# First-layer layer norm of chunks 1 and 2 issued ahead of the K and Q evictions, its rstd on ScalarE, w1/w2 loaded early, one DMA transpose per chunk

## The chip, the cores and the metric

The kernel runs on one core of a Trainium2 chip. The metric is the device time of one execution in microseconds (us); less is better. Line numbers such as L523 are lines of the kernel before.

## The reference

The input `x` has 2048 rows of 512 bf16 values. Four layers are applied to it in turn, each as x = x + f(layernorm(x)): attention, feed-forward, attention, feed-forward, with the same weights in both pairs.

```python
x = x + _A_ref(_layernorm(x), A_wqkv, A_wo)   # linear attention, 32 heads of 16
x = x + _B_ref(_layernorm(x), B_w1, B_w2)     # relu(h @ w1) @ w2, 512 -> 1376 -> 512
# ... and both once more
# in _A_ref: phi(t) = where(t > 0, t + 1, exp(t)) + 1e-6, on q and k
#   kv = sum_s phi(k) v;  z = sum_s phi(k);  out = (phi(q) kv) / (phi(q) z + 1e-6) @ wo
```

## The kernel before

The 2048 rows are 16 tiles of 128 rows, in four chunks of four tiles. Everything stays in SBUF; only the inputs and the result move to and from HBM. An attention layer has two stages.

**First stage.** For each tile: layer norm to `xn`, its transpose to `Tb`, the K projection (`a_k`: four 512-column matmuls into one PSUM bank); for each chunk: four Q projections (`a_q`, one bank each). Each K or Q bank is evicted by `phi_evac` in four instructions: on ScalarE (ACT) an identity with bias into `big` (L506) and an exp into `escr` (L508); on VectorE (DVE) a min into `emscr` (L510, "em") and a max in `big` (L516, "phi"). `escr` and `emscr` have 6 slots each (`NSCR`). From phi(K) come z (`a_z`, one-column matmuls) and G (`a_g`, 256-column matmuls of `xn` with phi(K); 128 matmuls in all).

**Second stage ("bar").** z becomes `Zc` (L557); `a_den` makes the denominators, whose reciprocals (L616, L618) are spread over partitions by 12 DMAs (`a_spread`, L628) and multiplied into phi(Q) (`a_pqs`, L637, "pqs"). G becomes KV (L590, two halves) and with `wo` becomes `Mf` (`a_m`, L597/L598; two pairs of matmuls called M pairs here). Then `a_fin_mm` computes the output ("fin"), L534 adds the residual, and `ln_next` makes the layer norm and the transposes of the next layer. The feed-forward layers (`b_h`, `b_out`) follow chunk by chunk.

**The first layer's norm.** Chunk 0 goes tile by tile (`ln_own`). For chunks 1 to 3, `ln_first` issues four `bn_stats` (L427, "bst"), four `bn_aggr` (L428), one `veps` (L435), then rstd as a power on GpSimd (POOL, L448), an `nbias` on DVE (L451) and four norms (L463, on ACT or DVE as the scheduler picks). Chunks 0 and 1 are transposed on TensorE (PE) through `transpose_pe` (L494, four matmuls a tile, "trp") and copied out of PSUM by ACT or DVE (L498/L499, "trev"); chunks 2 and 3 by a DMA transpose each (L479). In later layers all chunks go by DMA transpose; chunk 0 of the layer after an attention goes as two halves.

**What sets the order.** The code only lists operations with what they read and write, and a guessed cost. `_list_schedule` (L123) then simulates the engines and fixes one order per engine; each engine runs its list strictly in that order and waits on semaphores. A look-ahead of `WINDOW` operations in listing order, the guessed costs and the eight PSUM banks decide who goes first, so moving a call such as `ln_first` in the listing, or changing a guessed cost, re-orders all engines. `p1(t)` lists `ln_first(t + 1)` ahead of the K projections of chunk t. All DMAs, loads and transposes alike, are issued by SyncE (SP) on one queue. `ld_ff` (L382) holds the loads of `w1` and `w2` back until the transposed chunks 2 and 3 have landed; the first DMA transpose waits for `wk`, `wq`, `wv` and `wo` (`ALL_LOADS`).

```python
def p1(t):                                  # L823
    if first_layer and t + 1 < NCH:
        ln_first(t + 1)
        if t + 2 == NCH:
            ld_ff()
    for i in range(4 * t, 4 * t + 4):
        a_k(i)
```

Of the kernel before, what the change touches and what calls it, by code (L numbers as in the profile page):

```python
# [22 lines left out]
C_ACT_EXP = 495.0  # L23
C_DVE_FLEX = 600.0
# [13 lines left out]
C_POOL_NORM = 900.0  # L38
# [211 lines left out]
def build_kernel(nc, A_x, A_wqkv, A_wo, B_w1, B_w2, out, n_layers_pairs=2, K_STT=0, Q_STT=0, A_PE_CHUNKS=0, windows=None,  # L250
# [20 lines left out]
    with es:  # L271
# [25 lines left out]
        NSCR = 6  # L297
        escr = sb("escr", [128, NSCR, 512], BF16)
        emscr = sb("emscr", [128, NSCR, 512], BF16)
# [68 lines left out]
        def ld_x(t, lo=0):  # L368
            dma(lambda e, t=t: e.dma_start(xin[:, 4 * t + lo:4 * t + 4, :], x_v[:, 4 * t + lo:4 * t + 4, :]),
                [], [("xin", i) for i in range(4 * t + lo, 4 * t + 4)], 1500.0, "ld_x%d" % t)  # L370
        dma(lambda e: e.dma_start(xin[:, 0, :], x_v[:, 0, :]), [], [("xin", 0)], 100.0, "ld_x0a")
        wq_v = A_wqkv.rearrange("(c p) n -> p c n", p=128)
        ld_x(0, 1)
# [8 lines left out]
        def ld_ff():  # L382
            after = [("T", i) for i in range(4 * FIRST_PE_CHUNKS, NT)]
            dma(lambda e: e.dma_start(w1[:], B_w1.rearrange("(c p) n -> p c n", p=128)), after, [("w1",)], 4000.0, "ld_w1")
            dma(lambda e: e.dma_start(w2[:, 0:nfull, :], B_w2[0:nfull * 128, :].rearrange("(c p) n -> p c n", p=128)),
                after, [("w2a",)], 3800.0, "ld_w2a")
            if FLAST < 128:
                dma(lambda e: e.dma_start(w2[0:FLAST, NFC - 1, :], B_w2[nfull * 128:DFF, :]), after, [("w2b",)], 600.0, "ld_w2b")
        W2KEYS = [("w2a",), ("w2b",)] if FLAST < 128 else [("w2a",)]
        ALL_LOADS = [("wk",), ("wv",), ("wq",), ("wo",)]  # L390
# [39 lines left out]
        def ln_chunk(t, first):  # L430
            sl = slice(4 * t, 4 * t + 4)
            tl = range(4 * t, 4 * t + 4)
            if first:
                mean_ap = mv[:, sl, 0]
                g.add(DVE, lambda e: e.tensor_scalar(veps[:, sl], mv[:, sl, 1], 0.0, EPS, ALU.max, ALU.add),  # L435
                      [("var", i) for i in tl], [("veps", t)], C_DVE_SMALL, name="veps%d" % t)
            else:
                g.add(POOL, lambda e: e.tensor_scalar(mean[:, sl], s1[:, sl], -INV_D, None, ALU.mult),  # L438
                      [("s1", i) for i in tl], [("mean", i) for i in tl], C_POOL_SMALL, name="nmean%d" % t)
                g.add(POOL, lambda e: e.tensor_tensor(nm2[:, sl], s1[:, sl], mean[:, sl], ALU.mult),  # L440
                      [("s1", i) for i in tl] + [("mean", i) for i in tl], [("nm2", t)], C_POOL_SMALL, name="msq%d" % t)
                g.add(POOL, lambda e: e.tensor_scalar(nm2[:, sl], nm2[:, sl], D * EPS, None, ALU.add),
                      [("nm2", t)], [("nm2", t)], C_POOL_SMALL, name="msqe%d" % t)
                g.add(POOL, lambda e: e.tensor_tensor(var[:, sl], s2[:, sl], nm2[:, sl], ALU.add),
                      [("s2", i) for i in tl] + [("nm2", t)], [("var", i) for i in tl], C_POOL_SMALL, name="var%d" % t)
                g.add(POOL, lambda e: e.tensor_scalar(veps[:, sl], var[:, sl], INV_D, EPS, ALU.mult, ALU.max),
                      [("var", i) for i in tl], [("veps", t)], C_POOL_SMALL, name="veps%d" % t)
            g.add(POOL, lambda e: e.tensor_tensor(rstd[:, sl], veps[:, sl], nhalf[:, 0:4], ALU.pow),  # L448
                  [("veps", t), ("nhalf",)], [("rstd", t)], C_POOL_POW, name="rstd%d" % t)
            if first:  # L450
                g.add(DVE, lambda e: e.scalar_tensor_tensor(nbias[:, sl], mean_ap, -1.0, rstd[:, sl], ALU.mult, ALU.mult),  # L451
                      [("mean", i) for i in tl] + [("rstd", t)], [("nbias", t)], C_DVE_SMALL, name="nbias%d" % t)
            else:
                g.add(POOL, lambda e: e.tensor_tensor(nbias[:, sl], mean[:, sl], rstd[:, sl], ALU.mult),
                      [("mean", i) for i in tl] + [("rstd", t)], [("nbias", t)], C_POOL_SMALL, name="nbias%d" % t)

        def ln_norm(i, first):
            t = i // 4
            if first:
                src, rd = xin[:, i, :], [("xin", i), ("rstd", t), ("nbias", t)]  # L460
                alts = [(ACT, lambda e: e.activation(xn[:, i, :], src, ACTF.Identity, scale=rstd[:, i:i + 1], bias=nbias[:, i:i + 1]),
                         C_ACT_SB_AP),
                        (DVE, lambda e: e.tensor_scalar(xn[:, i, :], src, rstd[:, i:i + 1], nbias[:, i:i + 1], ALU.mult, ALU.add),  # L463
                         C_DVE_NORM_BF)]
                g.add_flex(alts, rd, [("xn", i)], name="norm%d" % i)
                return
            src = xres[:, i, :]
            if i % 4 == 2:
                g.add(ACT, lambda e: e.activation(xn[:, i, :], src, ACTF.Identity, scale=rstd[:, i:i + 1], bias=nbias[:, i:i + 1]),
                      [("xres", i), ("rstd", t), ("nbias", t)], [("xn", i)], C_ACT_SB_AP, name="norm%d" % i)  # L470
                return
            eng, cost = (POOL, C_POOL_NORM) if i % 4 == 3 else (DVE, 500.0)
            g.add(eng, lambda e: e.tensor_scalar(xn[:, i, :], src, mean[:, i:i + 1], rstd[:, i:i + 1], ALU.add, ALU.mult),  # L473
                  [("xres", i), ("rstd", t), ("mean", i)], [("xn", i)], cost, name="norm%d" % i)

        def transpose_chunk(t, extra_reads=(), parts=1):
            n = 4 // parts
            for i0 in range(4 * t, 4 * t + 4, n):
                dma(lambda e, i0=i0: e.dma_start_transpose(Tb[:, i0:i0 + n, :, :].rearrange("p i c t -> p (i c) t"),  # L479
                                                           xn[:, i0:i0 + n, :].rearrange("p i d -> p (i d)")),  # L480
                    [("xn", i) for i in range(i0, i0 + n)] + list(extra_reads),
                    [("T", i) for i in range(i0, i0 + n)], 2300.0 if parts == 1 else 1050.0, "tr%d_%d" % (t, i0 % 4),
                    issue=1200.0)

        def transpose_pe(i):
# [5 lines left out]
            def _emit(e, i=i):  # L491
                last = None
                for c in range(4):
# [5 lines left out]
                        (DVE, lambda e: e.tensor_copy(dst, psb()[:, :]), C_DVE_FLEX)],  # L499
                       [("ps", b)], [("T", i)], name="trev%d" % i)  # L500

        def phi_evac(b, dst_ap, dst_key, name, stt):
            s = scr_state["e"]
            scr_state["e"] = (s + 1) % NSCR
            if not stt:
# [4 lines left out]
            g.add(DVE, lambda e: e.tensor_scalar(emscr[:, s, :], escr[:, s, :], 1.0, 1e-6, ALU.min, ALU.add),  # L510
                  [("escr", s)], [("emscr", s)], C_DVE_BF4X, name=name + "_em")
            if stt:
                g.add(DVE, lambda e: e.scalar_tensor_tensor(dst_ap, psv[:, b, :], 1.0 + 1e-6, emscr[:, s, :], ALU.add, ALU.max),
                      [("ps", b), ("emscr", s)], [dst_key], C_DVE_PSUM, name=name + "_phi")
            else:
                g.add(DVE, lambda e: e.tensor_tensor(dst_ap, dst_ap, emscr[:, s, :], ALU.max),  # L516
# [283 lines left out]
        def ln_next(t, on_pe=False, parts=1):  # L800
# [5 lines left out]
            if not on_pe:  # L806
                tr_dma(t, parts)
# [217 lines left out]
```

## Time and profile before

| what | value |
|---|---|
| median of 3 runs | 291.74 us (291.61 to 292.29) |
| the profiled execution | 291.64 us, of which the span is 289.9 us |
| matmuls | 1696, PE busy 280.1 us (97% of the span) |
| ACT, DVE, POOL busy | 170.3, 139.6, 53.2 us |
| granted TensorE clock | 1.0 |
| DMA | 21.98 MB, of which 7.01 MB read from HBM |

PE's busy time hardly tells how much of the span is useful: matmuls are pipelined, and a row that stays open counts as busy. The spacing of the starts tells more: in a full stretch a 512-column matmul starts every 0.216 us (40 of them from 75.78 to 84.42 us) and a 256-column one about every 0.108 us. Where the starts lie further apart, PE waited. The views used below are the timeline of each engine (start, duration, line and count), the waits, and the time from issue to landing of each DMA.

### The profile page before, as it was taken

What the parts mean: (1) busy time and instruction counts of PE and PEld (TensorE: products, weight loads), DVE (VectorE), ACT (ScalarE), POOL (GpSimd) and SP (SyncE); (2) the same over time, 40 slices, a digit from 0 to 9 for tenths busy, and PEclk for the clock granted to TensorE, in tenths of its full rate; (3) what the DMA queues carried; (4) which work ended last, traced back from release to release, by engine and by line L of the source; (5) the groups of instructions that cost most, each with busy time, mean ns of one, the idle gap of its engine ahead of it and who ended that gap; (6) DMA issues with size and microseconds to landing.
All of it is one profiled execution on the core that took longest, in us unless ns stands there. A gap on an engine that the chain in (4) does not pass through costs nothing.

```text
span 289.9 us, 4431 instructions
## 1 busy us (share of the span) xinstructions
PE 280.1 (97%) x1696; PEld 143.4 (49%) x1696; DVE 139.6 (48%) x379; ACT 170.3 (59%) x352; POOL 53.2 (18%) x119
## 2 busy tenths in 40 slices
PE   7989899999899999999999999999999999999996
PEld 2456455644454454454455456674445445444444
DVE  4888856589800252260545387487971020020132
ACT  4888488738666285397554599843987605316000
POOL 5223100007800053040040320000880000000000
DMA  6900389661940007021003060281282005102012
GB/s 196 379 7 8 65 116 347 121 171 35 110 93 18 2 19 145 3 55 36 0 2 72 0 75 0 44 212 39 46 156 54 0 0 132 34 25 67 0 72 72
DMA packets 42790, 21.98 MB, mean 76 GB/s; under 512 B 34225, under 2 KB 40209, under 8 KB 42769
## 3 DMA queue, kind: packets, MB, share of 16 engines
q1 hardware_dynamic: 42768, 21.70, 32.6%
q8 instruction: 13, 0.21, 0.3%
q14 instruction: 9, 0.07, 0.1%
HBM read 7.01 MB, written 2.10 MB: 31 GB/s over the span
## 4 chain that ended last, share of the span: by engine, by line
PE 71%; DVE 11%; DMA 8%; ACT 4%; POOL 2%; SPq 1%; issue 1%; POOLq 0%
PE ps L523 71%; DMA Tb<-xn 4%; DVE xres L534 3%; DMA big<-rdc 3%; DVE bst L427 2%; POOL rstd L448 2%; ACT big L506 2%; DMA xin<-in_A_x_dram 1%; SPq L628 1%; ACT escr L508 1%; DVE big L637 1%; DVE xn L463 1%; ACT lnd L616 1%; DVE xn L473 1%; DVE big L516 1%
## 5 line engine op out<-in xcount | busy, mean ns | idle before, releaser
L523 PE MATMUL ps<-w,big 128*128 128x512 bf16 (+2 forms) x363 | 77.3, 372 | 0.0
L523 PE MATMUL ps<-Tb,w 128*128 128x512 bf16 x320 | 70.4, 379 | 0.0
L523 PEld LDWEIGHTS ps<-w,big 128*128 128x128 bf16 (+1 forms) x363 | 35.4, 98 | 40.7
L700 ACT ACTIVATE big<-ps 128x512 bf16<-128x512 f32 x74 | 44.1, 597 | 18.0 <-PE ps L523 17.9
L540 ACT ACTIVATE sqscr<-xres 128x512 bf16<-128x512 f32 x48 | 29.9, 624 | 33.6 <-DVE xres L534 33.4
L523 PEld LDWEIGHTS ps<-Tb,w 128*128 128x128 bf16 x320 | 30.8, 98 | 35.9
L506 ACT ACTIVATE big<-ps 128x512 bf16<-128x512 f32 x64 | 40.0, 626 | 9.6 <-PE ps L523 9.2
L534 DVE SCALAR_TENSOR_TENSOR xres<-ps,xres 128x512 f32<-128x512 f32 x32 | 21.1, 687 | 43.5 <-PE ps L523 43.5
L508 ACT ACTIVATE escr<-ps 128x512 bf16<-128x512 f32 x64 | 40.5, 633 | 0.0
L531 DVE TENSOR_TENSOR xin<-ps,xres 128x512 bf16<-128x512 f32 x15 | 10.4, 692 | 56.8 <-PE ps L523 56.8
L523 PE MATMUL ps<-big,xn 128*128 128x256 bf16 x256 | 31.8, 272 | 0.0
L523 PE MATMUL ps<-wqkv,Tb 128*128 128x512 bf16 x128 | 29.7, 379 | 1.0 <-DMA Tb<-xn 0.7
L510 DVE TENSOR_SCALAR emscr<-escr 128x512 bf16<-128x512 bf16 x64 | 18.5, 296 | 24.4 <-ACT escr L508 24.2
L523 PE MATMUL ps<-Tb,wqkv 128*128 128x512 bf16 x128 | 29.8, 379 | 0.1
L523 PE MATMUL ps<-Mf,big 128*128 128x512 bf16 x128 | 28.7, 379 | 0.0
L438 POOL TENSOR_SCALAR mean<-s 128x4 f32<-128x4 f32 x12 | 2.9, 239 | 136.8 <-DVE xres L534 136.8
L516 DVE TENSOR_TENSOR big<-big,emscr 128x512 bf16<-128x512 bf16 x64 | 26.9, 426 | 1.3
L523 PEld LDWEIGHTS ps<-big,xn 128*128 128x128 bf16 x256 | 23.8, 98 | 4.4 <-issue 0.9
L448 POOL TENSOR_TENSOR rstd<-veps,nhalf 128x4 f32<-128x4 f32 x15 | 17.7, 1177 | 20.6 <-DVE veps L435 19.6
L523 PEld LDWEIGHTS ps<-wqkv,Tb 128*128 128x128 bf16 x128 | 12.1, 98 | 15.2 <-ACT escr L508 1.2
L523 PEld LDWEIGHTS ps<-Mf,big 128*128 128x128 bf16 x128 | 12.2, 98 | 14.6 <-DVE Mf L598 0.8
L523 PEld LDWEIGHTS ps<-Tb,wqkv 128*128 128x128 bf16 x128 | 11.9, 98 | 13.5 <-ACT escr L508 0.4
(73 smaller groups left out, 198.8 us busy)
## 6 DMA issues: line engine op xcount, KB each, us to landing
big<-rdc SPq DMA_DIRECT2D x16, 128.0 KB, 2.7
big<-rdc SPq DMA_DIRECT2D x8, 256.0 KB, 4.7
wqkv<-in_A_wqkv_dram SPq DMA_DIRECT2D x3, 512.0 KB, 6.7
xin<-in_A_x_dram SPq DMA_DIRECT2D x3, 512.0 KB, 8.2
out_dram<-xin SPq DMA_DIRECT2D x3, 512.0 KB, 2.9
w<-in_B_w_dram SPq DMA_DIRECT2D x1, 1376.0 KB, 6.2
w<-in_B_w_dram SPq DMA_DIRECT2D x1, 1280.0 KB, 9.6
wo<-in_A_wo_dram SPq DMA_DIRECT2D x1, 512.0 KB, 10.2
```

Of the source, the lines that this page charges most:

```text
L427: g.add(DVE, lambda e: e.bn_stats(bst[:, i, :], xin[:, i, :]), [("xin", i)] + list(after), [("bst", i)], C_DVE_BNST, name="bnst%d" % i)
L438: g.add(POOL, lambda e: e.tensor_scalar(mean[:, sl], s1[:, sl], -INV_D, None, ALU.mult), [("s1", i) for i in tl], [("mean", i) for i in tl ...
L448: g.add(POOL, lambda e: e.tensor_tensor(rstd[:, sl], veps[:, sl], nhalf[:, 0:4], ALU.pow), [("veps", t), ("nhalf",)], [("rstd", t)], C_POO ...
L506: g.add(ACT, lambda e: e.activation(dst_ap, psv[:, b, :], ACTF.Identity, bias=1.0 + 1e-6, scale=1.0), [("ps", b)], [dst_key], C_ACT_PSUM, ...
L508: g.add(ACT, lambda e: e.activation(escr[:, s, :], psv[:, b, :], ACTF.Exp), [("ps", b)], [("escr", s)], C_ACT_EXP, name=name + "_exp")
L510: g.add(DVE, lambda e: e.tensor_scalar(emscr[:, s, :], escr[:, s, :], 1.0, 1e-6, ALU.min, ALU.add), [("escr", s)], [("emscr", s)], C_DVE_B ...
L516: g.add(DVE, lambda e: e.tensor_tensor(dst_ap, dst_ap, emscr[:, s, :], ALU.max), [dst_key, ("emscr", s)], [dst_key], 340.0, name=name + "_ ...
L523: last = e.matmul(o, l, r, start=st, stop=sp, skip_group_check=skip)
L531: g.add(DVE, lambda e: e.tensor_tensor(xin[:, i, :], psv[:, b, :], src, ALU.add), [("ps", b), skey], [("xin", i)], C_DVE_PSUM, name="resid ...
L534: g.add(DVE, lambda e: e.scalar_tensor_tensor(xres[:, i, :], psv[:, b, :], 0.0, src, ALU.add, ALU.add, accum_out=s1[:, i:i + 1]), [("ps", ...
L540: g.add(ACT, lambda e: e.activation(sqscr[:, q, :], xres[:, i, :], ACTF.Square, accum_out=s2[:, i:i + 1]), [("xres", i)], [("sqscr", q), ( ...
L700: g.add_flex([(ACT, lambda e, M=M, b=b, u=u: e.activation(unit_ap(u, M), psv[0:M, b, :], ACTF.Relu), C_ACT_PSUM), (DVE, lambda e, M=M, b=b ...
```

## The change

The layer norm of chunks 0, 1 and 2 is listed before the first K projection, that of chunk 3 after the K projections of chunk 0. In chunks 1 to 3 rstd is exp(-0.5 ln(var + eps)), two small activations on ACT in place of the power on POOL, and the norm is one DVE instruction (subtract mean, multiply by rstd) without `nbias`; chunk 1 goes in two halves of two tiles. `em` works in place in `escr`, which has 12 slots; `emscr` is gone. The loads of `w1` and `w2` are issued right after the other loads and wait for nothing. The first load brings two tiles of `x`, the second two. The DMA transpose of chunk 0 after an attention is one instruction, not two, and tile 3 of that chunk is normed on DVE, not on POOL. Some guessed costs differ.

```diff
-C_POOL_NORM = 900.0
+C_POOL_NORM = 1000.0
...
-        NSCR = 6
+        NSCR = 12
         escr = sb("escr", [128, NSCR, 512], BF16)
-        emscr = sb("emscr", [128, NSCR, 512], BF16)
...
-        dma(lambda e: e.dma_start(xin[:, 0, :], x_v[:, 0, :]), [], [("xin", 0)], 100.0, "ld_x0a")
+        dma(lambda e: e.dma_start(xin[:, 0:2, :], x_v[:, 0:2, :]), [], [("xin", 0), ("xin", 1)], 500.0, "ld_x0a")
...
-        def ld_ff():
-            after = [("T", i) for i in range(4 * FIRST_PE_CHUNKS, NT)]
-            dma(lambda e: e.dma_start(w1[:], B_w1.rearrange("(c p) n -> p c n", p=128)), after, [("w1",)], 4000.0, "ld_w1")
+        dma(lambda e: e.dma_start(w1[:], B_w1.rearrange("(c p) n -> p c n", p=128)), [], [("w1",)], 4000.0, "ld_w1")
...
-        ALL_LOADS = [("wk",), ("wv",), ("wq",), ("wo",)]
+        ALL_LOADS = [("wk",), ("wq",)]
...
+        def ln_part_first(lo, hi):
+            sl = slice(lo, hi)
+            tl = range(lo, hi)
+            g.add(DVE, lambda e: e.tensor_scalar(veps[:, sl], mv[:, sl, 1], 0.0, EPS, ALU.max, ALU.add),
+                  [("var", i) for i in tl], [("veps1", i) for i in tl], C_DVE_SMALL, name="veps%d" % lo)
+            g.add(ACT, lambda e: e.activation(var[:, sl], veps[:, sl], ACTF.Ln), [("veps1", i) for i in tl], [("lnv", lo)],
+                  C_ACT_TINY, name="lnv%d" % lo)
+            g.add(ACT, lambda e: e.activation(rstd[:, sl], var[:, sl], ACTF.Exp, scale=-0.5), [("lnv", lo)],
+                  [("rstd", i) for i in tl], C_ACT_TINY, name="rstd%d" % lo)
...
+        def ln_norm(i, first, urgent=False):
             if first:
+                g.add(DVE, lambda e: e.tensor_scalar(xn[:, i, :], xin[:, i, :], mv[:, i, 0:1], rstd[:, i:i + 1], ALU.subtract, ALU.mult),
+                      [("xin", i), ("mean", i), ("rstd", i)], [("xn", i)], C_DVE_NORM_BF, name="norm%d" % i)
                 return
...
-            eng, cost = (POOL, C_POOL_NORM) if i % 4 == 3 else (DVE, 500.0)
+            eng, cost = (POOL, C_POOL_NORM) if i % 4 == 3 and not urgent else (DVE, 460.0)
...
         def ln_first(t):
...
-            for i in range(4 * t, 4 * t + 4):
-                ln_stats_first(i)
-            ln_chunk(t, True)
+            step = 2 if t < FIRST_PE_CHUNKS else 4
+            for lo in range(4 * t, 4 * t + 4, step):
+                for i in range(lo, lo + step):
+                    ln_stats_first(i, [("veps1", lo - 1)])
+                ln_part_first(lo, lo + step)
...
-        ln_first(0)
+        for t in range(3):
+            ln_first(t)
...
                 def p1(t):
-                    if first_layer and t + 1 < NCH:
-                        ln_first(t + 1)
-                        if t + 2 == NCH:
-                            ld_ff()
                     for i in range(4 * t, 4 * t + 4):
                         a_k(i)
+                    if first_layer and t >= 0 and t + 3 < NCH:
+                        ln_first(t + 3)
...
-                    ln_next(t, t < A_PE_CHUNKS, 2 if t == 0 else 1)
+                    ln_next(t, t < A_PE_CHUNKS, t == 0)
```

## The prediction, made before the result was known

> **What bounds the kernel now.** I read the PE waits of the opening 76 us first, then the timelines of PE, DVE, ACT and SP over that stretch. From 75.1 to 182 us PE starts a 512-column matmul every 0.216 us without a gap, and again from 211.8 us to the end, so an edit pays there only if it shortens PE's own work, and none does. What can be won lies before 75 us and, less, around 193 to 212 us. PE's waits before 76 us (total, times, longest):
>
> ```profile
> PE ps L523 <- DMA Tb<-xn: 1.8, 2, 1.1
> PE ps L523 <- DVE big L516: 1.6, 2, 1.0
> PE ps L403 <- DVE wrm L396: 1.2, 1, 1.2
> PE ps L494 <- DVE xn L760: 0.8, 1, 0.8
> PE ps L523 <- DVE KVT L590: 0.5, 1, 0.5
> ```
>
> The warm-up aside, these sum to 4.7 us, and the spacing of starts shows a few tenths more. The cause sits earlier: on DVE the norms of chunk 2 start only at 26.01, because POOL's power took 2.2 us and DVE works on evictions between; SP can issue the transpose at 27.42, PE gets it at 31.86.
>
> ```profile
> 25.60 0.16 DVE L451 SCALAR_TENSOR_TENSOR nbias<-mv,rstd 128x4 f32<-128x4 f32 x1 [0.90 <-POOL rstd L448]
> 26.01 1.38 DVE L463 TENSOR_SCALAR xn<-xin,rstd,nbias 128x512 bf16<-128x512 bf16 x4
> ```
>
> PE fills most of that time with 40 matmuls of G (26.68), yet then has only K and Q work left, at ACT's pace:
>
> ```profile
> 26.68 4.53 PE L523 MATMUL ps<-big,xn 128*128 128x256 bf16 x40
> 31.86 1.90 PE L523 MATMUL ps<-wqkv,Tb 128*128 128x512 bf16 x8 [0.66 <-DMA Tb<-xn]
> 34.08 2.02 PE L523 MATMUL ps<-wqkv,Tb 128*128 128x512 bf16 x8 [0.31 <-ACT escr L508]
> ```
>
> Here the gap 33.59 to 34.08 is PE waiting for a bank that ACT evicts: two passes of 0.49 us, 0.98 us a tile, against PE's 0.864.
>
> **The change part by part.** I follow the changed kernel's fixed orders, with the spacing of starts from before's timelines: bst 0.59 us, bn_aggr and veps 0.09, em 0.20, phi 0.33, a bf16 norm 0.323 (four in 1.29), trev 0.38, an ACT pass 0.49, a K or Q tile 0.864, a trp tile 0.225, four z 0.10, a G matmul 0.1085.
>
> *First load.* Before, 128 KB landed 2.2 us after issue and the next 384 KB at 1.25 + 3.8 = 5.05, for which DVE idled 0.95 us. With 256 KB first, tile 0 comes at 3.0 to 5.0 (I take 3.4, near the small load's row), but tile 1 with it. Norm 1 then goes at 6.72 instead of 7.02, held by POOL's power for tile 1, which queues behind tile 3's square. The first K follows at 7.45 instead of 7.72; `wk` lands at 1.71 + 5.7 = 7.41, so no earlier.
>
> *Norms ahead of evictions, rstd on ACT.* Tile copies of chunk 0 end at 10.17 on DVE. From there to the last norm of chunk 2, DVE's list holds 10 bst (5.90), 8 bn_aggr (0.72), 4 em (0.80), 4 phi (1.33), 3 veps (0.27), 8 norms (2.58), 1 trev (0.38): 11.98 us, so 22.15. That holds if DVE never waits: chunk 1's `x` lands at 2.73 + 7.4 = 10.1, just in time. The small activation is not in the trace at this place; its nearest row is ACT L395, 128x2, 0.20 us. Lower bound 0.10 (the extra spacing of an accumulator read), upper 0.6 (a full-width pass). Six small ones (three pairs) lie ahead of chunk 2's norms, so 0.6 to 3.6; I take 0.20, 1.2 us. ACT stays in step: it ends tile 3's first pass at 12.2 (that K tile ends at 11.6), then come Ln, exp, small exp and three passes: 14.55; then 0.4 of small ones, three trev and five passes: about 19.0. DVE's veps are there at 12.0, 14.5 and 19.0. rstd of chunk 2 follows at 19.95, before DVE wants it at 20.9. If veps comes late, ACT's exp behind it waits, and with it a PSUM bank and PE. The removed power (2.1 to 2.2 us here) and `nbias` free POOL, which nobody else needs.
>
> *Twelve in-place slots.* DVE now evicts late: phi of K tiles 2 and 3 at 19.7 instead of about 15. With six slots ACT's exps would have to wait for them; with twelve none does, so it costs nothing. In place, em is taken at its 0.20; the trace has no in-place em, so bounds are 0.18 to 0.33 (phi, which is in place).
>
> *PE up to chunk 2's K.* From 7.45: 8 K and 8 Q tiles 13.82, six trp tiles 1.35, 16 z 0.43, 28 G 3.04: 18.64, so 26.1, and waits for tile copies of about 0.6 (0.2 ahead of K tiles 2, 6 and the trp of tile 5 each): 26.7. The transpose issued at 22.25 lands 4.4 later (its row before), at 26.65. PE and transpose meet; K of chunk 2 at 26.7 instead of 31.86.
>
> *w1/w2 early.* Unknown: what they do to that transpose. Before, the first loads (4.19 MB) moved at 345 to 409 GB/s from 6 to 14 us and were through at about 14.4; 2.82 MB more at 0.385 MB/us end at 21.7. The three w loads before needed 51.0 - 40.8 = 10.2 us from first issue to last landing; added to `wo`'s landing at 15.6 that gives at most 25.8. Lower bound of delay 0; upper 25.8 - 22.25 = 3.5. I take 0, since the data rate is the nearer row. The three issues (0.39, 0.50 and 2.53 us on SP) stand ahead of nothing until 22.25, and their old place at 40.8 to 44.3 freed nobody: the spreads start at 50.97.
>
> The Trainium skill, page "DMA: Bandwidth & Descriptors", section "Queues, rings and completion order", speaks against this edit: each DMA engine consumes descriptors in ring order, and SP has one ring on each. By that rule the transpose starts only behind the last w byte; with 25.8 as that moment the gain below would be nearly gone, with 21.7 nothing changes. No run here shows it yet.
>
> *From chunk 2's K to the second M pair* (61.17 before): 29.31 us, of which I count 26.7 of work (16 K and Q tiles 13.84, 72 G 7.81, 32 z 0.86, denominators, KV, M and the first 8 fin matmuls 4.2) and 2.6 idle. The changed order has 28 G and 16 z more to do there (3.47): 30.2. The bank gap goes, because z and G of chunk 1 now stand between the K tiles. Next late are phi of the last Q (0.76 before, at 55.45) and `KVT`, on DVE behind pqs that wait for the spreads (0.69 before; I keep 0.25, as 12 more G stand behind the first M pair). So 26.7 + 30.2 + 0.76 + 0.25 = 57.9: **3.3 us earlier**.
>
> *Next layer's chunk 0, from the second M pair.* Before: T landed at 75.05, 13.9 after it, while fin kept PE busy to 12.6 after. Now DVE has five pqs ahead of the first residual, which goes at +1.8 instead of +2.32; three more at 0.61 and the last's end: +4.24; POOL's chain as before (66.11 to 68.93, 0.18 behind): +7.24; three norms of 0.50 on DVE: +8.75, ACT's norm by +8.4. A whole-chunk transpose lands in 4.2 (79.67) to 5.4 (74.9); the halves here took 4.2 and 3.7 against 3.2 and 3.1 in the second pair, so I take 4.2 + 0.6: T at +13.6, **0.3 us won**, bounds -0.3 and +0.9. In the second pair: norms 205.87 + 1.5, landing 4.2, T at 211.6 against 211.70: 0, bounds -0.3 and +0.3.
>
> **Sum.** 3.3 + 0.3 + 0 = 3.6. The profiled execution took 291.64 us (span 289.9 and 1.74 around it), 0.1 under the median of 291.74. 291.64 - 3.6 = **288.0**, a span of about 286.3.
>
> **The rivals.** About 0.3%, or 0.9 us, is what a measurement can tell from no change.
> - *Half of it.* The 28 G that filled PE's wait before are moved behind chunk 2's K, and the lists of DVE, ACT and PE now follow each other tightly (three meetings within 0.1 us). If the idle after 31.86 stays in full and only the opening pays: 31.86 - (26.7 + 3.47) = 1.7, so 289.9. For it: DVE was busy 9.1 of 10 us from 10 to 30.
> - *No change.* A transpose at its slowest (5.6 at 35.2 us, 1.2 more) with the idle kept leaves 0.5; 291.1.
> - *Slower.* The w loads hold the first transpose. Up to a landing of 26.65 + 3.6 = 30.2 the gain is only eaten; from there on PE, whose list has K of chunk 2 next, stands idle. Landing 9.2 us after issue, as the small w load did behind the other two, gives 31.45: 4.8 late, less 3.6: 292.8. Against it: the loads should be through by then.
>
> **How the numbers follow.** Forecast (286.8 to 289.2) 0.50, half 0.23, no change 0.11, slower 0.16. Faster is the first two, 0.73. The low end takes the best bounds: 0.6 more at the layer norm, `KVT`'s 0.25 gone, 0.3 in the second pair: 286.8. The high end takes the w loads' bound, 288.0 + 3.5 = 291.5, which also holds the small activations' (2.4 more). What lies beyond is the slower case and a little of the forecast's lower side, under 2 in 10.
>
> **What would show it.** SP's first transpose at 22 to 23 us and landing within 4.4; chunk 2's K at 26 to 28; no PE wait for L508 near there; the second M pair near 58; the first residual right behind five pqs; POOL without powers before 60. Wrong if the first transpose lands after 30, if PE waits for trev or phi by over 1 us between 8 and 26, or if ACT stands in front of the small Ln.

## The result, and the profile after

| what | before | after |
|---|---|---|
| median | 291.68 us (291.35 to 292.29, 4 runs) | 289.50 us (289.34 to 289.69, 4 runs) |
| the profiled execution | 291.64 us, span 289.9 | 289.42 us, span 287.7 |
| POOL busy | 53.2 us | 46.6 us |
| DVE busy | 139.6 us | 138.7 us |

The ratio is 0.9923 [0.9906, 0.9941]: faster by 2.2 us, both by the medians and by the two profiled spans. The forecast was 3.6 us faster.

The lines of the changed kernel have other numbers: L515 is what L523 was (the helper that records PE's matmuls), L508 phi (was L516), L502 em (L510), L498 and L500 the two ACT passes (L506, L508), L459 the norm (L463), L472 the transpose (L479), L629 pqs (L637), L582 KV (L590), L526 the residual (L534). L433 and L435 are the new Ln and exp.

PE's waits before 76 us, of the changed kernel (total, times, longest):

```profile
PE ps L401 <- DVE wrm L394: 1.2, 1, 1.2
PE ps L486 <- DVE xn L752: 1.0, 1, 1.0
PE ps L515 <- DMA Tb<-xn: 0.9, 1, 0.9
PE ps L515 <- DVE big L508: 0.9, 1, 0.9
PE ps L515 <- DVE Tb L491: 0.3, 1, 0.3
PE ps L515 <- ACT Tb L490: 0.3, 1, 0.3
```

One of the two waits for a transpose is gone, and so is the wait for `KVT`; one of the two for phi (L508) is left, and two small ones for the tile copies are new. Before's table has a sixth row behind the five that the prediction shows:

```profile
PE ps L523 <- ACT escr L508: 0.3, 1, 0.3
```

That wait for a bank is gone too. Without the warm-up the six rows of before sum to 5.0 us with it, the changed kernel's to 3.4. That is 1.6 us, not 2.2: the rest is in the spacing of the starts, which the table of waits does not hold.

The wait for phi that is gone is the larger of the two, and the prediction did not follow it to its cause. In the kernel before, `nbias` of chunk 1 stands on DVE and waits for POOL's power, the phi of a K tile of chunk 0 stands behind it, and PE waits for that phi with z. DVE, then PE:

```profile
16.06 0.16 DVE L451 SCALAR_TENSOR_TENSOR nbias<-mv,rstd 128x4 f32<-128x4 f32 x1 [0.91 <-POOL rstd L448]
16.14 0.42 DVE L516 TENSOR_TENSOR big<-big,emscr 128x512 bf16<-128x512 bf16 x1
```

```profile
16.62 0.25 PE L523 MATMUL ps<-ones,big 128*128 128x1 bf16 x4 [0.98 <-DVE big L516]
```

The timeline of SP shows the three w loads, issued behind the other loads, and then the first two transposes (start, duration):

```profile
5.92 3.37 SPq L382 DMA_DIRECT2D w<-in_B_w_dram  x1
9.33 1.21 SPq L383 DMA_DIRECT2D w<-in_B_w_dram  x1
10.59 5.64 SPq L386 DMA_DIRECT2D w<-in_B_w_dram  x1
22.36 6.81 SPq L472 DMA_TRANSPOSE Tb<-xn  x2
```

The transpose of chunk 2 leaves at 22.36 instead of 27.42. It follows the norms on DVE:

```profile
20.97 1.37 DVE L459 TENSOR_SCALAR xn<-xin,mv,rstd 128x512 bf16<-128x512 bf16 x4
```

The line has no bracket at its end: DVE waited for nobody here, not for rstd either. The next view is PE from K of chunk 2 to the next layer's first matmuls, and the same place of the second pair. In the row at 27.36 the trace lacks the record of one of four matmuls; that tile began at about 27.14, as the first experiment's complete row shows. The row at 191.13 lacks the first of two as well, so that its wait is shorter by one matmul of 0.22 us: about 0.47.

```profile
27.36 0.81 PE L515 MATMUL ps<-wqkv,Tb 128*128 128x512 bf16 x3
...
53.20 0.40 PE L515 MATMUL ps<-big,Zc 128*32 128x512 bf16 x4 [0.86 <-DVE big L508]
...
58.77 0.60 PE L515 MATMUL ps<-wo,KVT 128*128 128x512 bf16 x2
...
72.63 0.85 PE L515 MATMUL ps<-w,Tb 128*128 128x96 bf16 x16 [0.90 <-DMA Tb<-xn]
...
191.13 0.38 PE L515 MATMUL ps<-wo,KVT 128*128 128x512 bf16 x1 [0.69 <-DVE KVT L582]
209.49 0.85 PE L515 MATMUL ps<-w,Tb 128*128 128x96 bf16 x16 [0.57 <-DMA Tb<-xn]
```

Four dates carry the gain from one end to the other. They are of the profiled executions; the gain is before less after.

| date | before | after | gain |
|---|---|---|---|
| K of chunk 2 begins (28 G and 16 z, 3.47 us, are moved behind it) | 31.86 | 27.14 | 4.7, of which 3.5 are only moved |
| second M pair | 61.17 | 58.77 | 2.40 |
| next layer's chunk 0 begins | 75.09 | 72.63 | 2.46 |
| the same in the second pair | 211.75 | 209.49 | 2.26 |

### The profile page after: what moved, and what is told of

Its sections match the earlier page's. It is cut to its first block, busy times and chain, and to the rows that moved or that the text cites. A ratio compares the mean times of both kernels' runs of the same rounds, so it can differ in the third digit from the quotient of the medians.

```text
span 287.7 us, 4410 instructions
## 1 busy us (share of the span) xinstructions
PE 278.1 (97%) x1677; PEld 143.6 (50%) x1696; DVE 138.7 (48%) x380; ACT 170.1 (59%) x359; POOL 46.6 (16%) x114
## 4 chain that ended last, share of the span: by engine, by line
PE 72%; ACT 12%; DMA 7%; DVE 5%; POOL 2%; issue 1%; SPq 0%; POOLq 0%
PE ps L515 71%; ACT big L498 5%; ACT escr L500 4%; DMA Tb<-xn 3%; DMA big<-rdc 3%; DVE xres L526 2%; DMA xin<-in_A_x_dram 1%; ACT lnd L608 1%; POOL rstd L451 1%; DVE bst L425 1%; ACT rdc L610 1%; DVE big L629 1%; DVE xn L468 1%; PE ps L486 0%; ACT Mf L589 0%
## 5 line engine op out<-in xcount | busy, mean ns | idle before, releaser
L515 PE MATMUL ps<-w,big 128*128 128x512 bf16 (+3 forms) x355 | 75.9, 373 | 0.4
L515 PE MATMUL ps<-Tb,w 128*128 128x512 bf16 x320 | 70.4, 379 | 0.0
L515 PEld LDWEIGHTS ps<-w,big 128*128 128x128 bf16 (+1 forms) x363 | 35.4, 97 | 40.8
L515 PEld LDWEIGHTS ps<-Tb,w 128*128 128x128 bf16 x320 | 30.8, 98 | 35.9
L498 ACT ACTIVATE big<-ps 128x512 bf16<-128x512 f32 x64 | 40.4, 631 | 7.6 <-PE ps L515 7.5
L526 DVE SCALAR_TENSOR_TENSOR xres<-ps,xres 128x512 f32<-128x512 f32 x32 | 21.1, 689 | 43.5 <-PE ps L515 43.5
L500 ACT ACTIVATE escr<-ps 128x512 bf16<-128x512 f32 x64 | 40.8, 637 | 0.0
L523 DVE TENSOR_TENSOR xin<-ps,xres 128x512 bf16<-128x512 f32 x15 | 10.4, 692 | 56.7 <-PE ps L515 56.7
L515 PE MATMUL ps<-big,xn 128*128 128x256 bf16 x256 | 31.8, 273 | 0.0
L502 DVE TENSOR_SCALAR escr<-escr 128x512 bf16<-128x512 bf16 x64 | 18.8, 301 | 24.4 <-ACT escr L500 24.3
L515 PE MATMUL ps<-Tb,wqkv 128*128 128x512 bf16 x128 | 29.8, 379 | 0.0
L515 PE MATMUL ps<-wqkv,Tb 128*128 128x512 bf16 x121 | 28.8, 380 | 0.9 <-DVE Tb L491 0.3
L515 PE MATMUL ps<-Mf,big 128*128 128x512 bf16 x126 | 28.7, 380 | 0.2
L508 DVE TENSOR_TENSOR big<-big,escr 128x512 bf16<-128x512 bf16 x64 | 26.4, 422 | 1.3
L515 PEld LDWEIGHTS ps<-big,xn 128*128 128x128 bf16 x256 | 23.8, 97 | 4.7 <-issue 0.9
L515 PEld LDWEIGHTS ps<-Mf,big 128*128 128x128 bf16 x128 | 12.3, 98 | 14.8 <-ACT Mf L589 0.6
L515 PEld LDWEIGHTS ps<-wqkv,Tb 128*128 128x128 bf16 x128 | 12.1, 98 | 14.0 <-DVE Tb L491 0.5
L515 PEld LDWEIGHTS ps<-Tb,wqkv 128*128 128x128 bf16 x128 | 12.1, 97 | 13.3 <-issue 0.4
L468 DVE TENSOR_SCALAR xn<-xres,mean,rstd 128x512 bf16<-128x512 f32 x26 | 13.4, 553 | 4.3 <-POOL rstd L451 4.2
```

Of the source, the lines that this page charges most:

```text
L498: g.add(ACT, lambda e: e.activation(dst_ap, psv[:, b, :], ACTF.Identity, bias=1.0 + 1e-6, scale=1.0), [("ps", b)], [dst_key], C_ACT_PSUM, ...
L500: g.add(ACT, lambda e: e.activation(escr[:, s, :], psv[:, b, :], ACTF.Exp), [("ps", b)], [("escr", s)], C_ACT_EXP, name=name + "_exp")
L502: g.add(DVE, lambda e: e.tensor_scalar(escr[:, s, :], escr[:, s, :], 1.0, 1e-6, ALU.min, ALU.add), [("escr", s)], [("escr", s)], C_DVE_BF4 ...
L508: g.add(DVE, lambda e: e.tensor_tensor(dst_ap, dst_ap, escr[:, s, :], ALU.max), [dst_key, ("escr", s)], [dst_key], 340.0, name=name + "_phi")
L515: last = e.matmul(o, l, r, start=st, stop=sp, skip_group_check=skip)
L523: g.add(DVE, lambda e: e.tensor_tensor(xin[:, i, :], psv[:, b, :], src, ALU.add), [("ps", b), skey], [("xin", i)], C_DVE_PSUM, name="resid ...
```

## The experiments

The theory after the result: the gain is the earlier transpose of chunk 2, so what moves DVE's norms forward pays, and early w loads, the single transpose and the number of slots bring nothing of their own. What is missing of the 3.6 us sits in named places: the opening, the denominators, the norm after the first attention, the second pair. Rivals are that the w loads do the work, that the parts only pay together, and that the missing part is not a queueing on DVE. In the table, dates are of one profiled execution each; the ratio is to the kernel before, run on the same chip.

| kernel | ratio to before | median, us | transpose issued | K of chunk 2 | second M pair | span |
|---|---|---|---|---|---|---|
| before | 1 | 291.68 | 27.42 | 31.86 | 61.17 | 289.9 |
| after | 0.9923 [0.9906, 0.9941] | 289.50 | 22.36 | 27.14 | 58.77 | 287.7 |
| e1_w_late | 0.9930 [0.9913, 0.9947] | 289.12 | 22.36 | 27.14 | 58.76 | 287.3 |
| e2_pow_pool | 0.9963 [0.9948, 0.9977] | 290.32 | 22.73 | 27.12 | 59.62 | 288.2 |
| e3_listed_late | 0.9957 [0.9941, 0.9973] | 290.14 | 26.05 | 30.45 | 59.61 | 288.6 |
| e4_slots6 | 0.9972 [0.9962, 0.9982] | 290.50 | 22.39 | 26.88 | 59.94 | 289.3 |
| e5_halves | 0.9913 [0.9900, 0.9926] | 288.84 | 22.29 | 27.07 | 58.80 | 287.3 |
| e6_listing_only | 0.9943 [0.9923, 0.9963] | 289.41 | 20.48 | 27.08 | 59.27 | 287.9 |
| e7_load_1_1_2 | 0.9925 [0.9911, 0.9939] | 289.13 | 23.23 | 27.79 | 59.54 | 287.7 |
| e9_act_rstd_only | 0.9954 [0.9941, 0.9968] | 290.04 | 26.44 | 30.86 | 59.71 | 288.5 |
| e10_phi_first | 0.9917 [0.9902, 0.9932] | 288.88 | 22.38 | 27.16 | 58.33 | 287.0 |
| e11_slots_6_6 | 0.9926 [0.9904, 0.9947] | 288.95 | 22.31 | 26.79 | 58.70 | 287.1 |
| e12_phi_first_halves | 0.9899 [0.9883, 0.9915] | 288.51 | 22.28 | 27.06 | 58.56 | 287.0 |

The kernel before had medians of 291.19 us beside e1 to e4, 291.36 beside e5 to e9, and 291.47 beside the last three, so kernels of different groups are compared by the ratio and not by the median.

### e1: the w loads wait for the transposes again

```diff
-        dma(lambda e: e.dma_start(w1[:], B_w1.rearrange("(c p) n -> p c n", p=128)), [], [("w1",)], 4000.0, "ld_w1")
...
+        def ld_ff():
+            after = [("T", i) for i in range(4 * FIRST_PE_CHUNKS, NT)]
...
                     if first_layer and t >= 0 and t + 3 < NCH:
                         ln_first(t + 3)
+                        ld_ff()
```

> The changed kernel with the w1/w2 loads held back again until the transposed chunks 2 and 3 have landed; the orders of PE, ACT, DVE and POOL are those of the changed kernel. My theory: the early loads neither give nor take anything, 289.2 to 289.8 us, first transpose issued near 22.4 us and landed 4.2 to 4.4 us later, as in the changed kernel. Rival A, the early loads hold the first transpose or the opening's loads back: 289.0 or less. Rival B, moving these loads away from 41 to 51 us is a part of the gain: 290.2 or more, with PE gaps after 41 us that the changed kernel has not.

The order on PE, ACT, DVE and POOL is that of the changed kernel. Its timeline of PE:

```profile
27.14 1.03 PE L517 MATMUL ps<-wqkv,Tb 128*128 128x512 bf16 x4
...
190.60 0.60 PE L517 MATMUL ps<-wo,KVT 128*128 128x512 bf16 x2 [0.18 <-DVE KVT L584]
```

Up to the next layer every date stands within 0.03 us of the changed kernel's, whether the w loads go early or late. Its median, 289.12, lies just under the theory's 289.2, but the kernel before was 0.5 us faster in that group too; the ratios, 0.9930 and 0.9923, are the same within their intervals. So no effect of the early loads is seen. The two spans differ by 0.4 us all the same, and one wait holds most of it: that for `KVT` in the second pair, 0.18 here and about 0.47 in the changed kernel. DVE's timelines, first of the changed kernel, then of e1, show why, at the same order:

```profile
189.76 0.76 DVE L629 TENSOR_TENSOR big<-big 128x512 bf16<-128x512 bf16 x2 [0.98 <-DMA big<-rdc]
190.44 0.42 DVE L582 TENSOR_TENSOR KVT<-ps,bmask 128x256 bf16<-128x256 f32 x1
```

```profile
189.44 0.76 DVE L631 TENSOR_TENSOR big<-big 128x512 bf16<-128x512 bf16 x2 [0.70 <-DMA big<-rdc]
190.12 0.42 DVE L584 TENSOR_TENSOR KVT<-ps,bmask 128x256 bf16<-128x256 f32 x1
```

KV stands on DVE behind pqs that wait for a spread, and that spread landed 0.3 us later in the one execution than in the other.

### e2: the powers back on POOL, all else as changed

```diff
-            g.add(ACT, lambda e: e.activation(var[:, sl], veps[:, sl], ACTF.Ln), ...
-            g.add(ACT, lambda e: e.activation(rstd[:, sl], var[:, sl], ACTF.Exp, scale=-0.5), ...
+            g.add(POOL, lambda e: e.tensor_tensor(rstd[:, sl], veps[:, sl], nhalf[:, 0:hi - lo], ALU.pow), ...
```

> The changed kernel with rstd of chunks 1 to 3 as one power on POOL instead of Ln and Exp on ACT. My theory: the power takes 1 to 2.2 us beside a busy DVE (2.07 and 2.20 us in the kernel before) against 0.6 to 0.9 us from veps to rstd on ACT, and the first norms of chunk 1 wait for it with PE behind them: the K of chunk 2 starts 0.5 to 1.5 us later than the 27.1 us of the changed kernel, 290.0 to 291.0 us. Rival, the listing alone carries the gain and where rstd is made does not matter: 289.2 to 289.8 us.

The time is as the theory had it, 0.8 us above the changed kernel by the medians and 1.2 us by the ratios, but the loss lies elsewhere. The transpose is only 0.37 us later and K of chunk 2 not at all. The loss comes with chunk 3: DVE waits for its power, four norms go, and phi, which stands behind them in DVE's list, is what PE then waits for. First DVE, then PE:

```profile
27.54 1.38 DVE L457 TENSOR_SCALAR xn<-xin,mv,rstd 128x512 bf16<-128x512 bf16 x4 [0.90 <-POOL rstd L433]
28.83 0.42 DVE L506 TENSOR_TENSOR big<-big,escr 128x512 bf16<-128x512 bf16 x1
```

```profile
30.05 0.25 PE L513 MATMUL ps<-ones,big 128*128 128x1 bf16 x4 [1.02 <-DVE big L506]
```

So once the norms are listed early, rstd on ACT is worth a wait of the evictions behind it, not an earlier transpose. It is the same chain as in the kernel before at 16.06: power, DVE, phi, PE.

### e3: the norms listed as before, all else as changed

```diff
-        for t in range(3):
-            ln_first(t)
+        ln_first(0)
...
+                    if first_layer and t + 1 < NCH:
+                        ln_first(t + 1)
                     for i in range(4 * t, 4 * t + 4):
                         a_k(i)
-                    if first_layer and t >= 0 and t + 3 < NCH:
-                        ln_first(t + 3)
```

> The changed kernel with the layer norm of chunk t+1 listed at p1(t) as before; rstd on ACT, 12 slots, early w loads and whole transposes stay. My theory: the listing is the gain; the first transpose is issued past 25 us again and the time is 290.6 to 291.7 us. Rival, rstd on ACT (no 2.2 us power between veps and norm) is the gain: transposes issued at 24 us or sooner and 289.2 to 290.0 us.

290.14 us is under the theory's range and above the rival's: beside the other parts the listing is worth 0.6 us by the medians and 1.0 us by the ratios, whose intervals just touch. Two signs of before's trace are back, the late transpose (26.05) and, on PE, the gap for a bank that ACT evicts:

```profile
32.76 2.10 PE L515 MATMUL ps<-wqkv,Tb 128*128 128x512 bf16 x8 [0.41 <-ACT escr L500]
```

### e6 and e9: each part alone, in the kernel before

e6 takes only the listing, e9 only Ln and exp on ACT.

```diff
 # e6, on the kernel before
-        ln_first(0)
+        for t in range(3):
+            ln_first(t)
...
-                    if first_layer and t + 1 < NCH:
-                        ln_first(t + 1)
-                        if t + 2 == NCH:
-                            ld_ff()
                     for i in range(4 * t, 4 * t + 4):
                         a_k(i)
+                    if first_layer and t + 3 < NCH:
+                        ln_first(t + 3)
+                        ld_ff()
```

> The kernel before with only the listing changed: layer norm of chunks 0, 1, 2 ahead of the K projections, of chunk 3 after those of chunk 0; rstd stays on POOL, six slots, late w loads, halves. After the first four experiments my theory is that the parts need each other (rstd on ACT back to POOL costs 0.5 to 0.9 us, six slots 1.0 to 1.6 us): alone the listing gives nothing, 0.998 to 1.003. Rival, the parts add up and the listing has its own 0.8 us: 0.996 to 0.9975.

```diff
 # e9, on the kernel before, in ln_chunk
+            if first:
+                g.add(ACT, lambda e: e.activation(var[:, sl], veps[:, sl], ACTF.Ln), [("veps", t)], [("lnv", t)], 200.0, ...
+                g.add(ACT, lambda e: e.activation(rstd[:, sl], var[:, sl], ACTF.Exp, scale=-0.5), [("lnv", t)], [("rstd", t)], 200.0, ...
...
```

> The kernel before with only rstd of chunks 1 to 3 made by Ln and Exp on ACT instead of the power on POOL; listing, nbias, slots and loads as before. Theory after the first four: this part alone is worth most of what is left with the late listing: first transpose near 26 us instead of 27.4, 0.9945 to 0.997. Rival, without the earlier listing the saved 1 to 2 us between veps and norm fall into time in which PE has G to do: 0.998 to 1.002.

e9 did as expected by its time. Only a part of it is the transpose, though, for which PE still waits 0.34 us (0.66 before). The larger part is the wait for phi at 16.62, which is gone, as PE's timeline shows with all four tiles of z in one row:

```profile
15.58 0.61 PE L528 MATMUL ps<-ones,big 128*128 128x1 bf16 x16
...
30.86 1.90 PE L528 MATMUL ps<-wqkv,Tb 128*128 128x512 bf16 x8 [0.34 <-DMA Tb<-xn]
```

With e6 my theory that the parts need each other fell, and its gain is above the rival's range as well: the listing alone gives 0.57%, e9 0.46%, and both with all else 0.77%. The intervals of e6 and of the changed kernel overlap, so that the whole beats the listing alone is likely and not shown. That they do not add up has two reasons in the traces: both take from the wait for chunk 2's transpose (0.34 is left in e9, nothing in e6), and the changed kernel has waits that neither of them has, 0.86 at the last denominators and two of 0.3 for tile copies. e6 issues the transpose even earlier than the changed kernel; what it pays is a wait of PE for chunk 1's norms, ahead of that chunk's transposes on PE. Its timelines of SP and PE:

```profile
20.48 10.00 SPq L479 DMA_TRANSPOSE Tb<-xn  x2
```

```profile
16.70 0.72 PE L494 MATMUL ps<-ident,xn 128*128 128x128 bf16 x8 [1.07 <-DVE xn L463]
...
27.08 3.62 PE L523 MATMUL ps<-wqkv,Tb 128*128 128x512 bf16 x16
```

K of chunk 2 begins at 27.08, as in the changed kernel, with PE's list deciding and not the transpose.

### e4 and e11: the slots

```diff
 # e4: six slots, em in place
-        NSCR = 12
+        NSCR = 6
...
 # e11: six slots for escr and six for emscr, as before
+        emscr = sb("emscr", [128, NSCR, 512], BF16)
...
-            g.add(DVE, lambda e: e.tensor_scalar(escr[:, s, :], escr[:, s, :], 1.0, 1e-6, ALU.min, ALU.add),
+            g.add(DVE, lambda e: e.tensor_scalar(emscr[:, s, :], escr[:, s, :], 1.0, 1e-6, ALU.min, ALU.add),
...
```

> The changed kernel with 6 in-place slots for the exps in place of 12. My theory: since DVE evicts late in the changed order, the scheduler has to let exps wait for slots and puts K and Q off: 290.0 to 291.0 us, with the second M pair 0.5 us or more later. Rival, the slots are only room that is not used: 289.2 to 289.8 us and nearly the same orders.

> The changed kernel with 6 slots for the exps and 6 separate ones for em, as before, in place of 12 in-place slots; the SBUF used is the same. Theory: six in-place slots cost 1.4 us because an in-place slot is held until phi, not only until em; with 6 and 6 the exps have more room and most of that cost is gone: 0.992 to 0.9945. Rival, twelve slots are what the early listing needs: 0.995 to 0.998.

Twelve slots in place are worth what six and six were. Six in place cost 0.5% by the ratios, as the theory of e4 had it. A slot is then held from the exp until phi, and the scheduler knows that; which operations it put off for it was not followed. It was not K of chunk 2: in e4 K of chunk 2 is early, and the time is lost behind it, on PE:

```profile
54.50 0.60 PE L515 MATMUL ps<-wo,KVT 128*128 128x512 bf16 x2 [1.01 <-DVE KVT L582]
...
74.20 0.85 PE L515 MATMUL ps<-w,Tb 128*128 128x96 bf16 x16 [1.49 <-DMA Tb<-xn]
```

### e5: two half transposes after the attention, tile 3 normed on POOL

```diff
-                ln_norm(i, False, urgent)
+                ln_norm(i, False)
...
-                    ln_next(t, t < A_PE_CHUNKS, t == 0)
+                    ln_next(t, t < A_PE_CHUNKS, 2 if t == 0 else 1)
```

> The changed kernel with the transpose of chunk 0 after an attention in two halves again and its tile 3 normed on POOL; PE's order is the changed kernel's. My theory: one transpose or two, the last piece lands within 0.3 us of the same moment, 0.990 to 0.9935 of the kernel before (the changed kernel: 0.9923). Rival, the single transpose is a part of the gain: 0.995 or more, with PE waits for the transposes of 0.4 us more in each pair of layers.

The single transpose brings nothing. With halves the next layer's chunk 0 begins at 72.44 instead of 72.63, after a wait of 0.68 us instead of 0.90. By the ratios e5 is 0.1% under the changed kernel, but the intervals overlap: if that part of the change does anything, it costs these 0.2 us.

### e7: the first x tiles as one, one and two

```diff
-        dma(lambda e: e.dma_start(xin[:, 0:2, :], x_v[:, 0:2, :]), [], [("xin", 0), ("xin", 1)], 500.0, "ld_x0a")
+        dma(lambda e: e.dma_start(xin[:, 0, :], x_v[:, 0, :]), [], [("xin", 0)], 100.0, "ld_x0a")
+        dma(lambda e: e.dma_start(xin[:, 1, :], x_v[:, 1, :]), [], [("xin", 1)], 300.0, "ld_x0b")
```

> The changed kernel with the first four tiles of x loaded as 1, 1 and 2 tiles instead of 2 and 2. Theory: in the changed kernel the first statistics wait until 3.79 us (3.01 before) for the larger first load, and the first K at 7.62 us is only 0.1 us ahead of the kernel before; with one tile first, the statistics start near 3.0, the first K at 7.0 to 7.3, and the time is 0.2 to 0.5 us under the changed kernel: 0.990 to 0.9917. Rival, the start is held by the weights of K or the warm-up, or the new order loses as much elsewhere: 0.992 to 0.995.

The rival was right: the start is held by K's weights, which one more load on the queue ahead of them delays. PE has nothing to do until then:

```profile
7.80 1.02 PE L516 MATMUL ps<-wqkv,Tb 128*128 128x512 bf16 x4 [2.01 <-DMA wqkv<-in_A_wqkv_dram]
```

The late start is not what the time shows, though: e7 is 0.77 us behind the changed kernel at the second M pair, 0.39 at the next layer (73.02) and level in the second pair (209.50), where its PE has no wait for `KVT`. A date of one execution is worth no more than such a wait.

### e10 and e12: the last phi ahead of the pqs

In the changed kernel DVE stands in a pqs that waits for a spread, and the last phi, ready since 51.6 (em at 51.31), stands behind it:

```profile
51.31 0.29 DVE L502 TENSOR_SCALAR escr<-escr 128x512 bf16<-128x512 bf16 x1
52.39 0.43 DVE L629 TENSOR_TENSOR big<-big 128x512 bf16<-128x512 bf16 x1 [0.79 <-DMA big<-rdc]
52.73 0.42 DVE L508 TENSOR_TENSOR big<-big,escr 128x512 bf16<-128x512 bf16 x1
```

e10 lists the pqs of chunk 0 as readers of the last phi and of the first half of KV, which puts both ahead on DVE. e12 does the same in e5.

```diff
-                      [("big", r), ("big", u)], [("big", u)], 340.0, name="pqs%d_%d" % (t, j))
+                      [("big", r), ("big", u)] + ([("big", pq_unit(k, NCH - 1)) for k in range(4)] + [("KVT", 0)] if t == 0 else []), ...
```

> The changed kernel with one more ordering rule: the multiplications of chunk 0 by the spread reciprocals (pqs) may go on DVE only after the phi of the last Q and after the first half of KVT. In the changed kernel DVE stands 0.79 us in front of the first pqs, waiting for its spread, with the last phi queued behind it; PE idles 0.86 us at the last denominators (0.6 to 1.0 in all kernels so far). Theory: that wait is a queueing on DVE and goes, in both attentions the M pairs come up to 0.8 us and 0.2 to 0.7 us earlier: 0.9875 to 0.9905 of the kernel before. Rival, the wait is only moved to the pqs, KVT or fin that now come later: 0.991 to 0.994.

> The ordering rule of the phi-first kernel together with the two half transposes and the norm of tile 3 on POOL, which measured 0.9913 on their own. Theory: the two edits touch different waits (last denominators; landing of the next layer's first transpose) and add: 0.1 to 0.2 us under the phi-first kernel alone, 0.987 to 0.990. Rival, with the fin stage earlier against the same spreads they share the time: same as the phi-first kernel or up to 0.3 us slower.

In e10 phi goes at 51.52 instead of 52.73, and PE's wait for the denominators is gone. Then DVE has the pqs still to do, and the spread has not come any earlier. DVE, then PE:

```profile
51.52 0.43 DVE L508 TENSOR_TENSOR big<-big,escr 128x512 bf16<-128x512 bf16 x1
52.83 0.42 DVE L582 TENSOR_TENSOR KVT<-ps,bmask 128x256 bf16<-128x256 f32 x1 [0.88 <-PE ps L515]
...
56.17 1.77 DVE L629 TENSOR_TENSOR big<-big 128x512 bf16<-128x512 bf16 x5 [0.52 <-DMA big<-rdc]
```

```profile
58.33 0.60 PE L515 MATMUL ps<-wo,KVT 128*128 128x512 bf16 x2 [0.28 <-DVE KVT L582]
...
71.83 0.85 PE L515 MATMUL ps<-w,Tb 128*128 128x96 bf16 x16 [0.54 <-DMA Tb<-xn]
```

The 0.86 us wait was a queueing on DVE, as the theory said, but at the second M pair only 0.4 us of it remain as a gain; the rest is a new wait for `KVT` and for spreads. In these two executions e10 is 0.80 us ahead at the next layer (71.83) and 0.65 in the second pair (208.84), but the ratio, 0.9917 against 0.9923, does not show that much, and it lies outside the theory's range and in the rival's. e12, with the halves as well, is the fastest of all, 0.9899, about 0.24% under the changed kernel by the ratios; the two intervals overlap, so that it beats the changed kernel is likely and not shown.

## Why the prediction was right and where its size was off

**What held.** Faster, and inside the range of 286.8 to 291.5, though 289.50 is above the forecast's own stretch (286.8 to 289.2). The mechanism held in part: the transpose of chunk 2 comes earlier and PE's wait for it is gone. "From there to the last norm of chunk 2 ... 11.98 us, so 22.15" gave an issue at 22.25; it was 22.36, since DVE needed 11.8 us but began 0.28 later, at 10.45. The landing 4.4 us after the issue was exact. "PE and transpose meet" was right to 0.4 us (landed at 26.76, K at 27.14), and so was "The bank gap goes": no PE wait for an ACT bank is left near 34. ACT never stood in front of the small Ln, as its timeline shows with no bracket at these rows or at the four like them up to 20.06:

```profile
12.78 0.22 ACT L433 ACTIVATE var<-veps 128x2 f32<-128x2 f32 x1
12.87 0.61 ACT L500 ACTIVATE escr<-ps 128x512 bf16<-128x512 f32 x1
13.35 0.23 ACT L435 ACTIVATE rstd<-var 128x2 f32<-128x2 f32 x1
```

The small activation takes 0.20 to 0.25 us in these six, but after five of them the next instruction starts 0.09 to 0.10 us later. The six cost some 0.6 us, at the low end of "0.6 to 3.6; I take 0.20, 1.2 us". The Trainium skill ("ScalarE: Activation LUTs", section "What ACT_TABLE_LOAD costs") gives 186 ns and 0.833 ns per element without pointer operands, and an overlap of 93 ns between neighbours. By estimate that is 0.19 us and a spacing of 0.095, close to the 0.20 to 0.25 and 0.09 to 0.10 of this trace.

**What it did not see.** "The cause sits earlier: on DVE the norms of chunk 2" explains the wait for the transpose. By the spacing of the starts that wait was 0.84 us (31.02 to 31.86). The wait for phi at 16.62, 1.11 us by the same measure (15.51 to 16.62), is larger and has nothing to do with chunk 2: it is POOL's power for chunk 1, with an eviction behind it. The sum counted it as gone without naming it, because it added up PE's work and a few named waits; that this came out is luck as far as the mechanism goes. Against the two stand 0.87 us of new waits for tile copies; with the first K 0.10 earlier that makes 1.2 us, the gain of the opening.

**The w loads.** "I take 0, since the data rate is the nearer row" was right: in e1, with the loads held back, the transpose is issued at 22.36 as well and lands 4.5 us later, here 4.4. The last w load was issued at 10.59 and landed 13.0 us after, at 23.6, so the estimate of 25.8 was too late and 21.7 too early. Its bytes were through before that: in windows of 0.05 us the DMA engines' busy share is 0 from 22.5 to 23.6 and rises then with the transpose's own bytes, 1.2 to 1.3 us after its issue. In e1 (issued at 22.36) and in the kernel before (27.42) they also begin 1.2 to 1.3 us after the issue. So the transpose met no w byte, and the rule of the Trainium skill ("DMA: Bandwidth & Descriptors", section "Queues, rings and completion order"), descriptors consumed in ring order, was not put to the test: by it too there was nothing left to wait for. There was about 1 us to spare, which the prediction's two estimates did not promise. The rival "Slower", which needed 4.8 us of it, did not come near.

**Where 1.4 us went.** The sum was 3.3 + 0.3 + 0; measured, from span to span, 2.40 + 0.06 - 0.20. The steps that were mis-sized:

- *The opening*, "8 K and 8 Q tiles ... so 26.1, and waits for tile copies of about 0.6 ...: 26.7". K of chunk 2 came at 27.14, 0.44 later. 0.17 is the first K (7.62, not 7.45), because the first load landed later: the first statistics went at 3.79, not 3.4. The rest is in the waits for tile copies: two, ahead of the K tiles at 10.26 and 18.70, of 0.87 us together by the spacing of the starts, instead of three of 0.2.
- *From chunk 2's K to the second M pair*, 31.63 us instead of 31.2 (57.9 less 26.7). The step "phi of the last Q (0.76 before, at 55.45)" kept the wait, and measured as that 0.76 was, by the spacing of the starts, it was 1.01 (52.19 to 53.20; the row's bracket has 0.86, against 0.60 before); "`KVT`" was to cost 0.25 and cost nothing. That leaves 0.4 us over the 30.2 counted as work (31.63 - 1.01 = 30.62). Of it, 0.2 stands around the denominators at 45.4 to 46.6, where the kernel before lost as much (48.7 to 49.9) and the sum let it go with the 2.6 of idle time, and 0.16 in two short stops behind the first K tiles (28.0 and 29.3); what these two wait for, the trace does not say. e10 shows the phi to be movable, and that about half of the place it frees is taken by the next in DVE's queue.
- *The layer norm*, "T at +13.6, 0.3 us won": T landed at about +13.8 and PE began at +13.86, 0.06 won. The first residual did not go "at +1.8" right behind five pqs but at +2.20, because PE's output was not there:

```profile
60.97 0.69 DVE L526 SCALAR_TENSOR_TENSOR xres<-ps,xin 128x512 f32<-128x512 f32 x1 [0.77 <-PE ps L515]
```

  I had looked at what DVE has ahead of it and not at what fin waits for, which is ACT's two copies of `Mf`, one behind the other (59.19 to 60.28; before, ACT made one and DVE the other, from 61.59 to 62.50). The issue of the transpose follows at +9.17, not +8.75; the landing, 4.6 us, was better than the 4.8 taken.
- *The second pair*, "0, bounds -0.3 and +0.3": it cost 0.20, within its bounds. The wait for `KVT` there was about 0.47, against 0.20 before, behind a spread (see e1). In the other kernels that have this wait it was 0.18 to 0.98. Why that spread lands later in one execution than in another is not settled.

Of the rivals, "Half of it" (289.9) came nearest by its number, but not by its mechanism. It held that the idle after chunk 2's K stays in full, 29.31 + 3.47 = 32.78 us to the second M pair; it was 31.63, so 1.15 us of that idle did go. The gain at the second M pair, 2.40, is 31.86 - (27.14 + 3.47) = 1.25 from the opening and 1.15 from behind it, against 1.7 and 1.6 in the forecast.

**Which part brings it.** Listing the norms earlier (e6) or taking the power off POOL (e9) each bring more than half of the gain alone. e6 ends the wait for the transpose; e9 ends the wait for phi behind the power and half of the other. Together they bring less than their sum, and by the ratios somewhat more than either, which the overlapping interval of e6 doesn't settle. The early w loads bring nothing that is seen (e1), the single transpose nothing or a little less (e5), the slots nothing as long as there are twelve in all (e4, e11). The guessed costs were not tried by themselves.

## What to carry to other kernels

Where an engine's list is fixed, moving the work that feeds a late transfer forward pays only as far as the next one in the list is ready: count the gain as the work that really leaves the path, after the work that only changes its place (3.5 of 4.7 us here). Follow every row of the table of waits to its cause, not the largest group alone: one slow small operation on another engine can stand in front of an eviction that has nothing to do with it. Two edits that shorten the same wait don't add up, so price them against that wait and not each alone. Before taking a gain at a residual, a copy or a phi, look both at what stands ahead of it on its own engine and at what its producer waits for.

## What the runs showed of the hardware that was not expected

- SP took 3.37, 1.21 and 5.64 us to issue the three w loads behind nine others, and 0.38, 0.50 and 2.29 us for the same in e6, at 32.86, long after those had landed. It held up SP alone; here nothing stood behind them until 22.36.
- The bytes of chunk 2's transpose began to move 1.2 to 1.3 us after its issue, with w loads ahead of it on the queue (after), without (e1) and in before's trace, and it landed after 4.4, 4.5 and 4.4 us. The last load ahead of it counted as landed only at 23.6, but its bytes had ended at 22.5. What a transpose does behind a load that still moves bytes, no run here shows.
- POOL's power on 128x4 took 2.06 and 2.19 us in two places of before's opening and 1.01 in a third (32.55); in e6 1.01, 1.31 and 2.19; in the later layers 1.04. A busy DVE alone does not explain it: the 1.01 us in e6 (at 14.88) ran beside a DVE that worked throughout, on `bn_stats` and `bn_aggr`, and in before's two long ones (13.96 and 23.38) DVE had em and phi only for the first 1.2 and 1.3 us and then waited. The cause was not tried.
